# Pairing the half blocks of two tiles' mixer products, moving some evictions, and a new order, in a fused recurrence-and-mixer kernel

## The chip, the cores and the metric

The kernel runs on one core of one Trainium2 chip. The metric is the device time of one execution in microseconds (us); lower is better. Shown are the median and the spread of runs, and for one execution the hardware profile.

## The reference

Two stages follow each other. The first is a recurrence over 768 time steps for 4 batches and 8 heads of 40 values, with a 40 x 40 state per head. The second mixes over the tokens and over the 320 channels (8 x 40).

```python
for t in range(S):                                   # per batch and head
    y[t] = rt @ state
    Sa = state @ at
    state = state * wt[None, :] - outer(Sa, bt) + outer(vt, kt)
x = y as (batch, token, 320)
theta = x @ w_theta
zr, zi = x * cos(theta), x * sin(theta)
u = x + w_tok_r @ zr + w_tok_i @ zi                  # over the 768 tokens of a batch
out = u + max(u @ w_ch, 0)
```

All inputs and the output are float32.

## The kernel before

The 768 tokens of a batch are cut into 6 tiles of 128, so there are 24 tiles, numbered through the batches. Work on a tile has these stages; names in brackets are the tiles and the lines of the profile.

*Loads.* SP's queue issues six loads of 160 KB a tile (w, k, b, a, v at L358, r for two tiles at L367), into buffers for 2 to 6 tiles. GpSimd's queue loads the mixer's weights (L705, L708: w_theta and w_ch, in two pieces each, as three blocks of 128 rows of which the last is half empty) and the token weights (L717).

*Preparation, `prep`.* ScalarE takes log w (`lw`, L382). TensorE forms the running sums of the logs (L389) and sums of the heads (L395), ScalarE their exponential (`ex`, L399). VectorE adds `lw` once more (`sx`, L402) and ScalarE takes the exponential of that (`we`, L406): the decays before and after a step. GpSimd multiplies k, b and a by them (`kb` L413, `ah` L417) and casts v and r (L422, L442). For the first two tiles VectorE and ScalarE do that work. TensorE transposes the results (L339, L450), ScalarE copies them out of PSUM (`kbT`, `aT`, `vT`, `nuT` at L342, `rT` at L454).

*Scores.* Four times a tile, 8 products over 64 rows each (two heads lie in the two halves of the rows, `mode=64`) form a 128 x 1024 score block in two PSUM banks (L467), and VectorE multiplies it by a triangular mask on its way to SBUF (L472): `psi`, `phi`, `lamv`, `lamu`.

*Recurrence.* With `psi` and `phi`, TensorE solves for the tile (L500, L506, L518), ScalarE copies out (`nx` L512, `nu` L522), and the state `gt` goes on to the next tile (L539; VectorE L550 or L558, GpSimd L554). This is the chain from tile to tile within a batch.

*Readout.* TensorE forms the tile's outputs (L602 to L611), VectorE scales them into `x` (L618).

*Theta.* Three transposes of `x` (L582; 320 columns padded to 384), a copy by ScalarE (`xT`, L342), three products with w_theta (L627), a copy (`th`, L637). After a batch's tiles, ScalarE takes sines and cosines (`cs`, L651; a table load when the function set changes) and GpSimd multiplies by `x` (`zr`, `zi`, L663).

*Mixing.* A row block takes 12 products over the batch's tokens (L680), VectorE adds `x` (`u`, L687). Then, as for theta, three transposes (L582), a copy (`uT`), three products with w_ch (L627), and VectorE's last step (`oo`, L696) ahead of the store (L699).

Nothing is scheduled at run time. Each operation is entered with `add` in the order of the program, and is then emitted in the order of the list `ORDER`, which was made beforehand; each engine takes its own operations strictly in that order. `HOMES` gives each PSUM use its bank, and `WARM` places warm-up products (L774) of TensorE ahead of some operations. The engine of each operation is fixed where it is entered.

Of the kernel before, what the change touches and what calls it, by code (L numbers as in the profile page):

```python
# [19 lines left out]
FROM_POOL = 4  # L20
ORDER = [
    0, 5, 3, 6, 2, 1, 19, 20, 4, 21, 12, 22, 23, 34, 26, 25, 80, 35, 30, 10, 31, 24, 7, 28, 79,
    29, 8, 27, 38, 36, 40, 9, 39, 32, 33, 14, 105, 41, 81, 42, 82, 13, 43, 53, 83, 15, 84, 226,
    54, 89, 55, 106, 11, 56, 107, 58, 90, 227, 57, 16, 91, 59, 37, 85, 60, 229, 62, 108, 18,
    111, 86, 64, 63, 17, 92, 65, 110, 74, 228, 68, 109, 69, 44, 114, 112, 93, 115, 70, 76, 61,
    116, 71, 135, 117, 45, 124, 113, 136, 66, 125, 137, 67, 87, 46, 138, 120, 72, 88, 94, 121,
    47, 73, 211, 95, 139, 122, 75, 126, 96, 140, 159, 143, 118, 127, 144, 160, 130, 123, 145,
    187, 161, 146, 119, 77, 188, 164, 128, 212, 162, 189, 48, 147, 213, 165, 129, 190, 163, 195,
    180, 168, 166, 196, 214, 148, 197, 131, 198, 170, 216, 191, 171, 141, 169, 217, 132, 192,
    215, 176, 174, 265, 220, 142, 78, 175, 218, 149, 199, 221, 133, 150, 266, 167, 200, 222, 49,  # L30
    172, 177, 223, 193, 267, 50, 241, 318, 230, 242, 268, 232, 173, 270, 231, 243, 269, 201,
    236, 319, 194, 244, 271, 202, 245, 320, 181, 246, 274, 219, 233, 183, 293, 275, 249, 272,
    294, 178, 182, 321, 250, 224, 295, 179, 322, 276, 97, 296, 237, 225, 251, 277, 302, 252, 98,
    203, 134, 303, 151, 456, 204, 282, 280, 286, 152, 323, 283, 297, 253, 238, 325, 254, 304,
    281, 247, 368, 255, 184, 324, 248, 298, 256, 372, 239, 327, 369, 305, 257, 299, 329, 328,
    186, 234, 273, 330, 185, 235, 258, 373, 339, 240, 457, 278, 370, 348, 340, 288, 337, 371,
    306, 458, 279, 459, 462, 343, 349, 284, 307, 502, 300, 285, 460, 350, 461, 503, 287, 351,
    308, 301, 463, 352, 504, 338, 465, 309, 289, 353, 310, 326, 466, 333, 354, 505, 311, 344,
    467, 355, 484, 468, 334, 485, 346, 471, 336, 508, 331, 472, 356, 335, 464, 345, 486, 551,
    156, 473, 332, 357, 469, 487, 552, 474, 470, 507, 488, 506, 492, 553, 374, 511, 489, 493,  # L40
    292, 554, 341, 512, 509, 290, 532, 342, 555, 358, 153, 494, 533, 513, 359, 534, 556, 495,
    514, 360, 535, 521, 361, 99, 536, 522, 496, 558, 157, 541, 347, 557, 537, 475, 377, 523,
    497, 562, 538, 158, 291, 498, 476, 499, 560, 477, 563, 510, 542, 539, 379, 500, 561, 527,
    524, 154, 540, 375, 501, 543, 376, 579, 478, 381, 544, 490, 515, 491, 566, 580, 382, 479,
    100, 516, 155, 581, 545, 383, 101, 582, 480, 396, 567, 517, 583, 568, 380, 529, 397, 546,
    518, 598, 584, 378, 398, 519, 588, 528, 569, 599, 585, 589, 399, 600, 400, 647, 530, 547,
    559, 601, 401, 520, 102, 590, 402, 525, 548, 603, 591, 586, 628, 587, 648, 602, 604, 564,
    629, 549, 526, 572, 565, 630, 605, 649, 570, 631, 607, 482, 550, 650, 653, 609, 571, 608,
    637, 483, 592, 652, 638, 481, 610, 632, 651, 593, 639, 617, 633, 578, 654, 403, 594, 640,
    656, 404, 577, 595, 52, 103, 596, 531, 205, 104, 619, 597, 618, 51, 658, 694, 641, 659, 208,  # L50
    657, 384, 642, 385, 613, 386, 620, 695, 634, 387, 696, 643, 614, 606, 644, 697, 664, 615,
    662, 709, 665, 675, 616, 388, 623, 676, 635, 389, 636, 655, 677, 206, 390, 678, 573, 660,
    207, 611, 661, 710, 663, 612, 679, 575, 712, 645, 711, 209, 680, 574, 666, 646, 210, 621,
    681, 391, 622, 405, 392, 624, 259, 684, 698, 724, 685, 262, 682, 667, 725, 686, 826, 726,
    408, 727, 409, 406, 683, 410, 687, 728, 827, 729, 393, 828, 701, 411, 625, 412, 829, 413,
    394, 699, 830, 730, 414, 705, 576, 688, 731, 700, 706, 415, 260, 395, 831, 416, 703, 689,
    626, 263, 261, 732, 365, 264, 417, 739, 733, 362, 420, 421, 315, 422, 704, 423, 424, 738,
    832, 425, 734, 690, 426, 713, 312, 691, 418, 715, 735, 692, 702, 714, 427, 835, 428, 693,
    707, 716, 833, 736, 836, 429, 708, 627, 742, 366, 737, 430, 837, 363, 367, 741, 838, 668,
    717, 747, 364, 841, 745, 854, 718, 444, 855, 671, 316, 743, 746, 445, 856, 317, 446, 740,  # L60
    719, 313, 842, 857, 447, 862, 751, 858, 847, 863, 448, 314, 744, 843, 859, 864, 669, 449,
    844, 834, 432, 749, 433, 434, 670, 872, 435, 450, 750, 436, 865, 437, 902, 849, 748, 873,
    903, 766, 438, 874, 753, 767, 897, 904, 875, 768, 905, 752, 866, 921, 839, 673, 867, 769,
    876, 770, 968, 674, 771, 879, 840, 906, 772, 848, 754, 877, 969, 907, 755, 970, 922, 672,
    756, 878, 971, 923, 911, 757, 924, 972, 758, 850, 974, 759, 912, 868, 925, 439, 760, 860,
    908, 419, 1017, 845, 913, 869, 721, 846, 909, 861, 440, 881, 910, 887, 883, 720, 882, 870,
    914, 1018, 884, 973, 888, 871, 407, 1019, 451, 891, 890, 722, 1020, 893, 880, 889, 977, 892,
    915, 452, 852, 978, 975, 885, 894, 853, 453, 886, 979, 942, 949, 980, 927, 916, 895, 950,
    989, 898, 896, 778, 951, 926, 773, 779, 952, 723, 780, 454, 781, 990, 958, 782, 899, 959,
    930, 928, 774, 441, 931, 783, 900, 442, 983, 932, 953, 933, 784, 917, 960, 431, 954, 918,  # L70
    936, 1064, 961, 919, 851, 955, 761, 1065, 920, 1022, 984, 762, 443, 937, 1066, 956, 986,
    962, 993, 929, 985, 938, 963, 987, 1021, 943, 1067, 934, 1023, 957, 763, 939, 935, 998,
    1068, 945, 964, 1024, 1026, 999, 965, 764, 940, 1027, 944, 988, 1028, 1000, 775, 976, 1001,
    966, 1029, 901, 776, 981, 967, 802, 941, 814, 982, 1002, 995, 1196, 815, 991, 1003, 1034,
    1038, 992, 1069, 816, 817, 818, 1108, 1004, 819, 1044, 1035, 1007, 803, 947, 804, 1008,
    1045, 1070, 994, 820, 1009, 1046, 1032, 1109, 1010, 805, 948, 1025, 1073, 1071, 996, 1047,
    1074, 1030, 1033, 806, 1048, 807, 1115, 1043, 1075, 1031, 1011, 1076, 808, 946, 1049, 1012,
    1036, 1083, 1050, 997, 1197, 1084, 1051, 790, 1198, 1054, 1005, 1039, 1242, 791, 1201, 1055,
    1199, 792, 1006, 793, 1037, 1200, 1052, 1202, 1089, 1243, 1094, 1244, 1203, 1056, 1053,
    1040, 1085, 1245, 1095, 1205, 1086, 1079, 1207, 1041, 1206, 794, 1072, 1096, 1208, 795,  # L80
    1057, 1113, 1097, 1224, 1080, 1222, 1225, 1257, 785, 1081, 1223, 1211, 796, 1213, 786, 1212,
    1226, 1217, 1082, 1013, 1058, 1227, 455, 1098, 1014, 1059, 1247, 1232, 1291, 1228, 1219,
    1214, 1099, 1258, 1233, 1204, 1246, 1292, 1248, 1015, 1042, 1293, 1229, 1100, 1259, 1294,
    1234, 1111, 1272, 1016, 1091, 1101, 1260, 1077, 1249, 1251, 1273, 787, 1218, 1078, 1235,
    1354, 1274, 1252, 1087, 1275, 1110, 1253, 765, 1339, 809, 788, 1102, 1220, 810, 1088, 1114,
    1254, 1060, 1340, 1061, 1355, 1341, 1267, 1276, 1103, 1356, 1261, 1250, 1277, 1263, 1357,
    1092, 1230, 1342, 1281, 1231, 1262, 1062, 1297, 1282, 1236, 1090, 1063, 1104, 1278, 1255,
    1237, 1105, 797, 1256, 1283, 1269, 1264, 1344, 798, 1312, 1343, 1209, 1313, 1106, 1345, 777,
    1210, 1284, 799, 1107, 789, 1314, 1346, 1295, 821, 1279, 1221, 1315, 800, 1215, 1383, 1265,
    1216, 822, 1321, 1268, 1350, 1298, 1322, 1348, 1351, 811, 1280, 1266, 1349, 801, 1384, 1296,  # L90
    1316, 1093, 1385, 1285, 1112, 1317, 1360, 1386, 1323, 1271, 1389, 812, 823, 1286, 1136,
    1116, 1300, 1318, 1270, 824, 1238, 1324, 1137, 1347, 1239, 1302, 1301, 813, 1138, 1120,
    1240, 1303, 1361, 1325, 1388, 1241, 1117, 1352, 1287, 1122, 1326, 1306, 1308, 1288, 1307,
    1392, 1299, 1353, 1160, 1118, 1393, 1304, 1161, 1309, 1305, 1162, 1119, 1364, 1319, 1123,
# [96 lines left out]
def kernel(  # L191
# [91 lines left out]
    for i, t in sorted(to_zero, key=lambda e: e[0]):  # L283
        nc.vector.memset(t, 0.0)
# [526 lines left out]
```

## Time and profile before

| | before |
|---|---|
| median of 3 runs | 206.26 us (204.8 to 206.72) |
| profiled execution, span from first to last instruction | 204.3 us (the page gives no other time of it) |
| TensorE: matmuls / weight loads busy | 191.4 / 156.3 us |
| VectorE busy | 174.4 us |
| ScalarE busy | 151.6 us |
| GpSimd busy | 127.0 us |
| granted TensorE clock, mean | 1.000 |
| DMA, moved | 30.82 MB, mean 151 GB/s |

A busy time is the union of an engine's instructions; matmuls overlap each other, and their ends are modelled, so TensorE's busy share says less than the distance from one start to the next. An engine that is idle and isn't waited for costs nothing. The chain that ended last follows the execution back from its end, at each step to what released it.

### The profile page before, as it was taken

How to read it: one execution, taken by the hardware profiler on the slowest of the kernel's cores; microseconds unless marked ns; L12 is line 12 of the kernel's file. 1: busy time of each engine (PE TensorE's matmuls, PEld its weight loads, DVE VectorE, ACT ScalarE, POOL GpSimd, SP SyncE). 2: the span in 40 equal slices, each digit the busy share in tenths (PEclk: the TensorE clock that was granted, in tenths of full speed). 3: DMA queues.
4: the chain of work that ended last, by engine and by line, in shares of the span. 5: the costliest groups of instructions: out<-in, count | busy, mean ns of one | idle time of the engine just before them, and what ended most of it. 6: DMA issues, size and time to landing. Idle time of an engine off the chain costs nothing.

```text
span 204.3 us, 8134 instructions
## 1 busy us (share of the span) xinstructions
PE 191.4 (94%) x3372; PEld 156.3 (77%) x3372; DVE 174.4 (85%) x277; ACT 151.6 (74%) x364; POOL 127.0 (62%) x186
## 2 busy tenths in 40 slices
PE   7878789888999999999899999999999999999993
PEld 6756668667878888887678888788888878777771
DVE  7499899799999998996886989999999987956543
ACT  3577668799999977868667859898999967756021
POOL 3015178559999996659959918548987953635000
PEclk9999999999999999999999999999999999999999
DMA  6989899999899999979999889797999400012223
GB/s 135 198 158 197 155 172 167 182 159 195 139 186 204 155 256 191 147 141 178 170 191 207 169 176 186 169 181 131 220 199 192 96 3 5 0 67 78 87 77 116
DMA packets 134181, 30.82 MB, mean 151 GB/s; under 512 B 125824, under 2 KB 134144, under 8 KB 134144
## 3 DMA queue, kind: packets, MB, share of 16 engines
q1 hardware_dynamic: 131712, 27.54, 68.8%
q0 software_dynamic: 2432, 2.77, 8.6%
q8 instruction: 26, 0.43, 0.9%
q14 instruction: 11, 0.09, 0.1%
HBM read 29.13 MB, written 3.93 MB: 162 GB/s over the span
## 4 chain that ended last, share of the span: by engine, by line
PE 71%; DVE 8%; DMA 8%; SPq 5%; ACT 2%; issue 2%; POOL 1%; DVEq 0%; ACTq 0%; POOLq 0%
PE ps_s L680 19%; PE ps_s L339 12%; PE ps_d L467 10%; PE ps_s L627 9%; SPq L358 4%; DMA wrow_i<-in_moe_w_tok_i_dram 4%; PE ps_s L582 4%; DMA raw_v<-in_v_dram 3%; PE ps_s L450 2%; PE ps_s L539 2%; DMA raw_r<-in_r_dram 2%; PE ps_s L518 2%; PE ps_s L611 2%; PE ps_s L725 2%; PE ps_s L506 2%
## 5 line engine op out<-in xcount | busy, mean ns | idle before, releaser
L413 POOL TENSOR_TENSOR kb<-raw_kb,ex 128x320 bf16<-128x320 f32 x44 | 37.6, 868 | 10.0 <-ACT ex L399 4.3
L680 PE MATMUL ps_s<-zr,wtok_r 128*128 128x320 bf16 x144 | 41.1, 299 | 0.0
L680 PE MATMUL ps_s<-zi,wtok_i 128*128 128x320 bf16 x144 | 41.0, 299 | 0.0
L472 DVE TENSOR_TENSOR psi<-ps_d,mask_p 128x1024 bf16<-128x1024 f32 x24 | 29.2, 1216 | 4.3 <-PE ps_d L467 4.1
L472 DVE TENSOR_TENSOR lamu<-ps_d,mask_p 128x1024 bf16<-128x1024 f32 x24 | 29.1, 1215 | 3.0 <-PE ps_d L467 2.9
L472 DVE TENSOR_TENSOR phi<-ps_d,mask_n 128x1024 bf16<-128x1024 f32 x24 | 29.2, 1215 | 0.8 <-PE ps_d L467 0.8
L472 DVE TENSOR_TENSOR lamv<-ps_d,mask_p 128x1024 bf16<-128x1024 f32 x24 | 29.0, 1215 | 0.5 <-PE ps_d L467 0.4
L417 POOL TENSOR_TENSOR ah<-raw_a,we 128x320 bf16<-128x320 f32 x22 | 19.1, 868 | 8.0 <-issue 5.0
L663 POOL TENSOR_TENSOR zr<-cs,x 128x320 bf16<-128x320 f32 x23 | 18.0, 791 | 6.7 <-DVE oo L696 4.2
L663 POOL TENSOR_TENSOR zi<-cs,x 128x320 bf16<-128x320 f32 x23 | 17.9, 790 | 6.2 <-ACT cs L651 6.2
L467 PE MATMUL ps_d<-aT,kbT 64*128 64x128 bf16 x384 | 17.3, 217 | 1.8 <-ACT aT L342 1.1
L342 ACT COPY uT<-ps_s 128x192 f32<-128x192 f32 x24 | 7.6, 324 | 14.6 <-PE ps_s L582 14.6
L554 POOL TENSOR_TENSOR gt<-sum,ex 128x320 bf16<-128x320 f32 x13 | 9.4, 725 | 13.3 <-DVE sum L550 13.3
L680 PEld LDWEIGHTS <-wtok_r 128*128 128x128 bf16 x144 | 14.0, 97 | 4.1
L687 DVE TENSOR_TENSOR u<-ps_s,x 128x320 bf16<-128x320 f32 x24 | 11.6, 486 | 5.9 <-PE ps_s L680 5.7
L342 ACT COPY kbT<-ps_s 128x512 f32<-128x512 f32 x24 | 14.3, 594 | 3.1 <-PE ps_s L339 2.9
L680 PEld LDWEIGHTS <-wtok_i 128*128 128x128 bf16 x144 | 14.1, 98 | 3.3
L442 POOL CAST r<-raw_r 128x640 bf16<-128x640 f32 x11 | 8.0, 725 | 11.7 <-ACT lw L382 9.7
L696 DVE SCALAR_TENSOR_TENSOR oo<-ps_s,u 128x320 f32<-128x320 f32 x24 | 11.6, 484 | 4.2 <-PE ps_s L627 3.5
L467 PEld LDWEIGHTS <-kbT 64*128 64x128 bf16 x384 | 11.5, 94 | 4.8 <-ACT kbT L342 1.9
L339 PE MATMUL ps_s<-ident,kb 128*128 128x128 bf16 x192 | 14.7, 219 | 0.4 <-POOL kb L413 0.2
L609 PE MATMUL ps_s<-kb,lamv 128*128 128x40 bf16 x192 | 15.1, 180 | 0.0
(119 smaller groups left out, 590.8 us busy)
## 6 DMA issues: line engine op xcount, KB each, us to landing
raw_w<-in_w_dram SPq DMA_DIRECT2D x24, 160.0 KB, 4.2
raw_r<-in_r_dram SPq DMA_DIRECT2D x24, 160.0 KB, 3.6
raw_a<-in_a_dram SPq DMA_DIRECT2D x24, 160.0 KB, 3.5
raw_kb<-in_b_dram SPq DMA_DIRECT2D x24, 160.0 KB, 3.8
raw_kb<-in_k_dram SPq DMA_DIRECT2D x24, 160.0 KB, 3.9
raw_v<-in_v_dram SPq DMA_DIRECT2D x24, 160.0 KB, 4.2
out_dram<-oo SPq DMA_DIRECT2D x24, 160.0 KB, 2.4
wrow_i<-in_moe_w_tok_i_dram POOLq DMA_DIRECT2D x6, 192.0 KB, 5.3
```

The lines of the kernel that those rows point to most:

```text
L339: nc.tensor.transpose(out=dst[:, c:c + 128], in_=pair(src, g), identity=ident)
L342: nc.scalar.copy(out=out.bitcast(FP32), in_=in_)
L413: lambda j=j: (nc.vector if fast else nc.gpsimd).tensor_tensor(out=paired(kb[:, j])[:, :, :, 0:D], in0=natural(raw_kb[s4][:, j]), in1=invW ...
L417: lambda: (nc.vector if fast else nc.gpsimd).tensor_tensor(out=paired(ah)[:, :, :, 0:D], in0=natural(raw_a[i % 6]), in1=Wi, op=ALU.mult),
L467: nc.tensor.matmul(t[:, q, g, :], lhsT=lhs[rows(q), g * 128:(g + 1) * 128], rhs=rhs[rows(q), g * 128:(g + 1) * 128], start=True, stop=True)
L472: add("DVE", kindm, i, lambda: nc.vector.tensor_tensor(out=dst.rearrange("p a b c -> p (a b) c"), in0=ps(p).rearrange("p a (g c) -> p (a g ...
L609: nc.tensor.matmul(o, lhsT=lamv[:, p, g, :], rhs=kb[:, 0, h, 0:D], start=first, stop=False, skip_group_check=True)
L627: nc.tensor.matmul(dst, lhsT=lhs[:, kt, :], rhs=rhs[:, kt, :], start=kt == 0, stop=kt == 2)
L663: nc.vector if fast else nc.gpsimd).tensor_tensor(
L680: nc.tensor.matmul(ps(pk)[:, 0:DM], lhsT=wtok[nm][:, s, j * 128:(j + 1) * 128], rhs=zs[c][:, s], start=n == 0 and c == 0, stop=n == NT - 1 ...
L687: add("DVE", "uadd", q, lambda: nc.vector.tensor_tensor(out=u[:, 0:DM], in0=ps(pk)[:, 0:DM], in1=x[:, 0:DM], op=ALU.add), 488, [pk, ("x", ...
L696: add("DVE", "oo", q, lambda: nc.vector.scalar_tensor_tensor(out=oo, in0=ps(ck)[:, 0:DM], scalar=0.0, in1=u[:, 0:DM], op0=ALU.max, op1=ALU ...
```

## The change

Pairs: the outputs `x` of two tiles in turn lie side by side in one tile `xp` of 640 columns, and so do `u` (`up`). 640 columns are five transposes of 128: two blocks of the first tile, two of the second, and one that holds the last 64 columns of the first tile in its upper half of rows and the first 64 of the second in its lower half. One copy takes all five out of PSUM. Each tile then has two full products, and the shared block gives each of the two a product over 64 rows, from its half of the rows into its own PSUM bank. The mixer weights are held in five blocks to match: the first three as before, with the lower half of the third now filled with rows 0 to 63, and rows 64 to 319 as two more. They take four loads each instead of two. Tiles 22 and 23 go alone, as before, from `xs` and `us`.

Decay sums: for tiles 0 to 6 (`EXCLUSIVE = 7`) a TensorE product of `lw` with the strict triangle `mask_p` gives the earlier sums themselves, and ScalarE takes their exponential from PSUM; VectorE's `sx` falls away for them.

Alternatives: an operation can carry a second way of doing it on another engine (`alts`), and a list `PICK` says which take it. A masked eviction's second way is a plain copy with sign on ScalarE followed by a triangular select on GpSimd, in place. In the built kernel 21 of 96 go that way (9 `phi`, 8 `lamv`, 3 `psi`, 1 `lamu`). 33 copies out of PSUM go to VectorE (13 `nuT`, 8 `vT`, 5 `kbT`, 4 `aT`, 3 `uT`) and 5 of `xT`; 7 of 12 token-weight copies go to ScalarE; 14 z products are on VectorE (2 before); 3 more casts of v are on ScalarE.

The lists `ORDER`, `HOMES` and `WARM` are new (63 warm-up products, 65 before). Sines are taken for tiles 0 to 3, then 4, then 5 of the last batch (0 to 2, 3 and 4, then 5 before). Part of the memsets move from VectorE to GpSimd.

The core of the diff:

```diff
+        for n in PICK:
+            self.ops[n].eng, self.ops[n].fn = self.ops[n].alts[0]
...
+        if i < EXCLUSIVE:
+            xk = ("ps", "cx", i)
+            add("PE", "cx", i, lambda: nc.tensor.matmul(
+                ps(xk)[:, 0:DM], lhsT=mask_p[:, 0, :], rhs=lw[:, :, 0:D], start=True, stop=True),
+                mm(320), [("lw", s2)], [xk], new=(xk, 1), tail=tail(320))
+            add("ACT", "ew", i, lambda: nc.scalar.activation(
+                out=we, in_=ps(xk)[:, 0:DM], func=AF.Exp), 455, [xk], [kw], table="lnexp")
...
         add("DVE", kindm, i, lambda: nc.vector.tensor_tensor(
-            out=dst.rearrange("p a b c -> p (a b) c"),
-            in0=ps(p).rearrange("p a (g c) -> p (a g) c", c=128),
-            in1=mask.to_broadcast([128, 2 * G, 128]), op=ALU.mult), 1217, [p], [dkey])
+            out=flat, in0=whole(), in1=mask.to_broadcast([128, 2 * G, 128]), op=ALU.mult),
+            1217, [p], [dkey], alts=(("ACT", lambda: nc.scalar.mul(
+                out=flat, in_=whole(), mul=sign)),))
+        add(None, "sel", i, None, 0, [dkey], [dkey], alts=(("POOL", lambda: nc.gpsimd.affine_select(
+            out=flat, in_=flat, pattern=[[0, 2 * G], [1, 128]], compare_op=ALU.is_gt,
+            fill=0.0, base=0, channel_multiplier=-1)),))
...
+    def blocks_of(t):
+        if t.shape[-1] == 3 * 128:
+            return [t[:, m:m + 128] for m in (0, 128, 256)]
+        return [t[:, m:m + 128] for m in (0, 128, DM + 64, DM + 192, 256)]
...
+    def mixed(kind, q, lhs, wt, wkeys, lkey, at="tile"):
+        for c in range(1 if alone(q) else 2):
+            pk = ("ps", kind, q + c)
+            def go(c=c, pk=pk):
+                n = 3 if alone(q) else 2
+                for kt in range(n):
+                    nc.tensor.matmul(ps(pk)[:, 0:DM], lhsT=lhs[:, c * n + kt, :],
+                                     rhs=wt[:, 3 * c + kt, :], start=kt == 0,
+                                     stop=kt == 2, skip_group_check=n == 2)
...
+        def both():
+            for c in range(2):
+                nc.tensor.matmul(ps(("ps", kind, q + c))[:, 0:DM], lhsT=lhs[rows(c), 4, :],
+                                 rhs=wt[rows(c), 2, :], start=False, stop=True,
+                                 skip_group_check=True)
...
-    def mix3(dst, lhs, rhs):
-        for kt in range(3):
-            nc.tensor.matmul(dst, lhsT=lhs[:, kt, :], rhs=rhs[:, kt, :],
-                             start=kt == 0, stop=kt == 2)
```

## The prediction

> **What bounds the kernel now.** I read the page first, then the table by ten-microsecond stretches, the chain that ended last, the timeline where TensorE changes between forms of product, the groups by line, and the order in which each engine and queue gets its instructions.
>
> Two lines of the page's slices, TensorE and VectorE (each digit is the busy share of 5.1 us):
>
> ```profile
> PE   7878789888999999999899999999999999999993
> DVE  7499899799999998996886989999999987956543
> ```
>
> The stretches (busy us of PE, PEld, DVE, ACT, POOL, then granted clock, DMA share, GB/s):
>
> ```profile
> 10.00:20.00 10.00, 7.67 (x152) 6.00 (x144) 9.24 (x12) 7.71 (x19) 3.59 (x5) 1.00 0.91 174
> 40.00:50.00 10.00, 8.77 (x181) 7.00 (x179) 9.47 (x11) 9.65 (x21) 7.58 (x11) 1.00 0.98 181
> 60.00:70.00 10.00, 9.88 (x190) 8.01 (x188) 10.00 (x16) 9.25 (x21) 9.46 (x15) 1.00 1.05 185
> 150.00:160.00 10.00, 10.00 (x204) 8.61 (x202) 9.79 (x16) 9.46 (x23) 8.00 (x11) 1.00 1.01 200
> 160.00:170.00 10.00, 10.00 (x157) 7.98 (x156) 8.76 (x11) 7.24 (x18) 7.55 (x12) 1.00 0.05 15
> ```
>
> There are three regimes. Until about 50 us the DMA engines are full and TensorE has holes: it waits for tiles to arrive. From 50 us on TensorE has none to speak of, while VectorE, ScalarE and GpSimd are nearly full too until 80 us. After 160 us the loads are over and TensorE works off a backlog. The clock is 1.00 throughout.
>
> A busy TensorE is not proof, so I price its steps from two lines of the chain (start, length, work) and three of the timeline (start, length, operation):
>
> ```profile
> 90.16 0.45 PE ps_s L339 x8
> 165.92 1.91 PE ps_s L680 x14
> ```
>
> ```profile
> 161.75 0.33 PE L582 MATMUL ps_s<-ident,x 128*128 128x128 bf16 x3
> 162.01 0.62 PE L467 MATMUL ps_d<-aT,kbT 64*128 64x128 bf16 x16
> 162.56 0.62 PE L339 MATMUL ps_s<-ident,kb 128*128 128x128 bf16 x8
> ```
>
> A transpose of 128 columns takes 0.056 us (0.45/8), a product of 320 columns 0.136 (1.91/14). The score products use 64 rows each and run two at a time. Three transposes from 161.75 should make room at 161.92; the scores start at 162.01, and their 16 (8 pairs of 0.053, 0.43) hold the next work until 162.56. So one stretch of 64-row work costs about 0.09 on entry and 0.12 at the end, together 0.2 us more than its products. Steps of 80 columns take 0.035, shorter ones 0.025.
>
> Adding TensorE's order at these steps gives 181.9 us for the kernel before. Set against the last L518 product of a tile, whose tile-0 time is 12.7 us with 6.6 us of work ahead of it, the lag (time less work) is 6.1 us at tile 0, 14.9 at tile 5 (49.4 us), 16.0 at tile 8 (65.0) and 18.4 at tile 23 (178.9). After that product 21.4 us of work are left and the span is 204.3, so 4.0 us are lost at the end. The lag arises almost wholly before 50 us; afterwards TensorE's own work is the time. That is the sum I use: 181.9 + 18.4 + 4.0 = 204.3. The page gives no other time of this execution; the three runs shown lie 0.5 to 2.4 us above the span, their median 206.26 about 2.0 above, and I add 2.0 at the end.
>
> **The change on TensorE.** Eleven pairs of tiles, in theta and channel mixer each, make 22 pair operations; tiles 22 and 23 keep the old way. (1) Five transposes replace six: 22 x 0.056 = -1.2 us. (2) A pair had six full products; it now has four, and two half blocks of 64 rows side by side. 44 full products go (-6.0), 22 side-by-side pairs come (+3.0): -3.0. That two 320-column halves overlap is not in this trace; the bounds are 0.136 a pair (as the score pairs overlap) and 0.272 (not at all, total 0.0). I take the first, since the score products use the same row halves and separate PSUM banks, and so do these. (3) Each pair would open a 64-row stretch, but in the built order 18 of the 22 stand beside score products; stretches go from 64 to 58: 6 x 0.2 = -1.2. (4) Seven early decay sums become a product (L389 form): +7 x 0.136 = +1.0. (5) Two fewer warm-up products: -0.1. Sum -4.5; added up in the built order TensorE has 177.4 us instead of 181.9.
>
> The Trainium skill (TensorEngine Tiling, Key Properties) says that changing the tiling mode drains TensorE, which speaks against a change that adds 22 mode changes of its own. The rows agree, with 0.2 us a stretch. By that rule with each pair alone the term would be +4.4 instead of -1.2, and the whole TensorE sum +1.1; the built order, with 18 joined, is why I don't take it.
>
> **The other engines.** *VectorE*: 21 of 96 masked evictions (L472, 1.215 us) leave, -25.5; 7 decay sums (L402, 0.482), -3.4; 7 of 12 token-weight copies (L729, 0.551), -3.9; about -3 of memsets, most of them in the first 5.4 us. It gains 13 nuT, 8 vT, 5 kbT, 4 aT and 8 xT/uT evictions, priced by L729 (768 words of 16 bits in 0.551; 512 then between 0.37 in proportion and 0.55; I take 0.42, with a fixed part), +17.6; 12 of the z products (0.485), +5.8; one ah, +0.5. Sum -11.9. *ScalarE*: 21 evictions of 1024 columns; copies of 256 and 512 words take 0.378 and 0.594, so 0.16 + 0.85 a thousand gives 1.03 each, +21.6; 48 xT/uT copies become 18 (-8.1); the copies that VectorE took -12.5; seven token copies +3.4; two table loads fewer -2.6; small ones +1.9: +3.7. *GpSimd*: 21 masks by select, in no row at this size. Bounds: the rate of the cast (320 in 0.451, 640 in 0.725), 1.05 us, and that of the two-input product L413 (320 in 0.868), up to 2.6; the 128-column select that builds masks takes 0.29, and scaled up from there it is 1.1 to 1.7. I take 1.35: +28; four more weight loads and the memsets +5, twelve z products fewer -9.5, the rest -2.5: about +21, to 148 of some 200 us. By the Trainium skill (GPSIMD Engine Reference, Performance versus the Vector engine: 1.03 to 1.8 cycles an element for one input at 1.2 GHz) a select would be an estimated 0.9 to 1.5 us; the sum would stay as it is.
>
> None of these is counted as time: GpSimd's 21 us fall in a queue that was idle for 77, ScalarE's 3.7 in 53 idle. That cover fails where selects queue ahead of kb and ah products in 50 to 80 us, where GpSimd was 96% busy; but in its built queue the first five selects stand ahead of that stretch, where it was idle for 22 of 50 us, and the first batch's z products come before the sixth, with four of twelve given to VectorE.
>
> What a moved mask does add is latency. A mask was one operation of 1.215 us; now it is 1.03 on ScalarE, then a select of 1.05 to 2.6: +0.9 to +2.4 on the way to x0 (psi) or nu (phi), 12 such in all, with every later eviction on ScalarE and kb product on GpSimd queued behind. VectorE's shorter queue gives some of it back. I put the part that TensorE feels at +1.0 (bounds: -2, the shorter queue wins; +10.4, all twelve show at the low price).
>
> **The load-paced start.** There a saved product is only a longer hole, so what counts is when a tile's data are there. Of 144 loads of 160 KB on SP's queue, in the old order the last that batch 0 (tiles 0 to 5) needs for its recurrence is the 42nd, issued at 39.0 us; in the new one the 39th. At 0.93 us a load that is -2.8. Past that the places match within two (tile 7: 49th in both; tile 9: 59th and 61st). Against it, theta's weights are loaded twice (200 KB more early, at 170 GB/s +1.2). The new first tile also doesn't wait behind memsets for its decay:
>
> ```profile
> 4.70 0.45 DVE L284 MEMSET x<- 128x32 uint32 x10
> 5.41 0.43 DVE L402 TENSOR_TENSOR sx<-ps_s,lw 128x320 f32<-128x320 f32 x1
> ```
>
> but that second is swallowed by the loads behind it. Net -1.6 at tile 5 (bounds 0 and -4): its L518 at 47.8 instead of 49.4.
>
> **Sum.** From tile 5 on: 177.4 - 34.3 = 143.1 us of TensorE work (147.4 before), 3.5 of later lag (18.4 - 14.9), 4.0 at the end, +1.0 for the masks. 47.8 + 143.1 + 3.5 + 4.0 + 1.0 = 199.4 of span, 4.9 less; with 2.0 around it **201.4 us**.
>
> **Rivals.** *A, more gain*: VectorE, full from 10 to 80 us, is what holds the early tiles, not the loads; then its 4.2 us less work up to tile 6's x (58.0 to 53.8 by the rows) come through in place of the 1.6, and the shorter queue pays for the masks: 201.4 - 2.6 - 1.0 = 197.8. For it: 9.2 to 10 us busy in each of those stretches. Against: DMA share 0.91 to 1.05 in the same ones. *B, slower*: the moved psi and phi masks are on the recurrence, and TensorE, which takes its work in order, stands at L506 and L518 for each. At the low price 12 x 0.87 = 10.4 instead of 1.0: 210.8. At 0.08 a mask it is the forecast's 1.0; past 0.67 us a mask (1.0 + 4.9 of gain + 2.1 over 12) the kernel is slower than before by over 1%. For it: twelve waits in a strict order with only a few us of slack on three full engines. Against: in the old trace DVE is as full there, so a mask waited in its queue anyway. *C, no change by the loads*: DMA share averages 0.96 up to 160 us; if the loads set tile 23's time, TensorE's saving becomes idle time: 204.3 + 2.0 = 206.3, and the 0.4 MB more of weights would take another 2.4 at 170 GB/s only if no buffer wait of the loads absorbed them. Against: tile 23's last load is issued at 156.9 us and its L518 comes 22 us later, where tile 7 needed 11 (46.2 to 57.7), so there are some 10 us of slack. *D, the change doesn't do what it says*: half blocks don't overlap, +3.0: 204.4.
>
> **Chances.** Forecast 0.48 (own range 199 to 204), A 0.18, B 0.15, C 0.12, D 0.07. A measurement of this kernel can tell about 1%, 2.1 us. Faster by over 1% (under 204.2): forecast and A, 0.66. Within 1%: C and D, 0.19. Slower: B, 0.15. The range reaches into A below and halfway to B above: 195.5 to 208.
>
> **What would show it.** Right: two L627-like half products starting within 10 ns of each other and taking 0.136 a pair; VectorE near 163 us busy; selects of 1.1 to 1.7; TensorE's work near 177 with tile 5's nu product near 48 us, lag under 19 at the last. Wrong: waits of L506 or L518's weight loads on the selects of over 5 us in total (B); the last nu tracking the last load's landing (C); selects over 2 us with kb products behind them.

## The result and the profile after

The changed kernel takes 211.99 us (median, 210.14 to 213.62), the old one 206.24 beside it: a ratio of 1.028 (95% interval 1.021 to 1.036). It is slower, where 201.4 was forecast. The profiled execution took 211.76 us, 210.1 of them span.

TensorE and VectorE in the slices of the changed kernel's page (each digit the busy share of 5.25 us):

```profile
PE   6997897998879898899999999999999899997993
DVE  4279897999978997789899879799989997468353
```

```profile
40.00:50.00 10.00, 8.74 (x173) 6.72 (x170) 9.02 (x12) 9.04 (x20) 7.60 (x11) 1.00 0.98 180
50.00:60.00 10.00, 8.78 (x180) 6.99 (x177) 9.29 (x12) 8.14 (x21) 7.65 (x11) 1.00 0.98 165
60.00:70.00 10.00, 8.29 (x167) 7.21 (x167) 8.73 (x13) 9.42 (x21) 8.77 (x13) 1.00 1.04 202
80.00:90.00 10.00, 8.77 (x185) 7.45 (x182) 7.35 (x11) 7.70 (x20) 8.58 (x14) 1.00 1.18 204
150.00:160.00 10.00, 9.51 (x216) 8.31 (x212) 9.12 (x14) 9.51 (x22) 9.74 (x14) 1.00 0.54 135
160.00:170.00 10.00, 9.38 (x169) 7.22 (x166) 9.69 (x14) 9.27 (x18) 8.14 (x11) 1.00 0.41 91
```

These are six of the stretches, with columns as in the prediction. The old kernel's TensorE had next to no holes from 50 us on (9.88 busy at 60 to 70 us); the changed one has them until 90 us (8.29 busy at 60 to 70 us) and again from 150 us. Until 90 us no other engine is full in the stretches shown (at most 9.42 of 10); from 150 to 170 us GpSimd and VectorE nearly are (9.74, 9.69). So TensorE waits, for several things in turn. Its waits, over the whole span (us in total, times, longest):

```profile
PE ps_s L357 <- POOL kb L394: 1.8, 4, 0.7
PE ps_d L496 <- ACT aT L360: 1.7, 2, 1.1
PE ps_s L765 <- DVE oo L788: 1.2, 1, 1.2
...
PE ps_d L496 <- ACT phi L508: 1.0, 1, 1.0
```

The chain that ended last, between 50 and 92 us (start, length, work), shows what stands behind GpSimd's ah and kb: loads.

```profile
57.99 3.99 DMA raw_a<-in_a_dram
62.05 0.10 issue
62.15 0.86 POOL ah L394
...
77.14 3.49 DMA raw_kb<-in_b_dram
80.67 0.08 issue
80.77 0.87 POOL kb L394
```

The halves do overlap. A pair of half products is a line with x2 in TensorE's timeline; the next product starts 0.25 us after it, one step of 0.136 and the changes of form:

```profile
189.62 0.31 PE L662 MATMUL ps_s<-wch,uT 64*128 64x320 bf16 x2
189.87 0.31 PE L765 MATMUL ps_s<-zr,wtok_r 128*128 128x320 bf16 x1
```

Among the groups (busy us, mean ns) there is one surprise, VectorE's mixer products at L751. The moved masks (L508, L510) are shown beside them:

```profile
L751 DVE TENSOR_TENSOR zr<-cs,xp 128x320 bf16<-128x320 f32 x8 | 6.8, 869 | 0.0
L751 DVE TENSOR_TENSOR zi<-cs,xp 128x320 bf16<-128x320 f32 x4 | 2.6, 657 | 0.0
L751 DVE TENSOR_TENSOR zi<-cs,xs 128x320 bf16<-128x320 f32 x2 | 2.0, 1016 | 0.0
L510 POOL TENSOR_SCALAR_AFFINE_SELECT phi<-phi 128x1024 bf16<-128x1024 bf16 x9 | 10.4, 1150 | 0.9 <-ACT phi L508 0.9
L508 ACT ACTIVATE phi<-ps_d 128x1024 bf16<-128x1024 f32 x9 | 9.3, 1037 | 0.3 <-PE ps_d L496 0.3
```

The same instruction took 0.48 to 0.49 us in the old trace, where VectorE did two of them:

```profile
L663 DVE TENSOR_TENSOR zi<-cs,x 128x320 bf16<-128x320 f32 x1 | 0.5, 491 | 0.8 <-ACT cs L647 0.8
L663 DVE TENSOR_TENSOR zr<-cs,x 128x320 bf16<-128x320 f32 x1 | 0.5, 479 | 0.0
```

**The prediction's sum, refilled.** I add up TensorE's order at the prediction's steps, with 0.1 us for each change between full and 64-row products, in both traces: 182.6 us before, 178.0 after, so 4.6 less (forecast 4.5; the prediction's own count was 181.9 and 177.4). The rest is the lag.

| part of the span, us | forecast | after | before, same count |
|---|---|---|---|
| tile 5's last nu product | 47.8 | 49.9 | 49.4 |
| TensorE's work behind it | 143.1 | 143.6 | 147.9 |
| lag gained from there to tile 23's (masks with it) | 4.5 | 10.8 | 3.1 |
| lost at the end | 4.0 | 5.8 | 3.9 |
| span | 199.4 | 210.1 | 204.3 |

Of the 10.8, 6.7 arise between tiles 5 and 11 (49.9 to 90.9 us), 2.5 between tiles 19 and 23 (150.0 to 181.3 us).

### The profile page after: what moved, and what is told of

It reads as the page before. It is cut to its first block, busy times and chain, and to the rows that moved or that the text cites. A ratio compares the mean times of both kernels' runs of the same rounds, so it can differ in the third digit from the quotient of the medians.

```text
span 210.1 us, 8112 instructions
## 1 busy us (share of the span) xinstructions
PE 192.0 (91%) x3355; PEld 153.9 (73%) x3355; DVE 170.3 (81%) x268; ACT 155.5 (74%) x335; POOL 144.8 (69%) x204
## 4 chain that ended last, share of the span: by engine, by line
PE 51%; ACT 13%; DMA 11%; DVE 10%; issue 5%; POOL 5%; SPq 4%; POOLq 0%; DVEq 0%; ACTq 0%
PE ps_s L765 15%; PE ps_s L357 8%; PE ps_d L496 6%; PE ps_s L652 4%; DMA raw_kb<-in_b_dram 3%; DMA raw_kb<-in_k_dram 3%; SPq L374 2%; DMA wth<-in_moe_w_theta_dram 2%; PE ps_s L620 2%; DMA raw_a<-in_a_dram 2%; PE ps_s L662 2%; DVE zr L751 2%; DVE oo L788 2%; POOL kb L394 1%; PE ps_s L555 1%
## 5 line engine op out<-in xcount | busy, mean ns | idle before, releaser
L506 DVE TENSOR_TENSOR psi<-ps_d,mask_p 128x1024 bf16<-128x1024 f32 x21 | 25.6, 1217 | 4.4 <-PE ps_d L496 4.3
L394 POOL TENSOR_TENSOR ah<-raw_a,we 128x320 bf16<-128x320 f32 x21 | 18.5, 880 | 6.4 <-DMA raw_a<-in_a_dram 1.7
L506 DVE TENSOR_TENSOR lamv<-ps_d,mask_p 128x1024 bf16<-128x1024 f32 x16 | 19.5, 1216 | 0.3 <-PE ps_d L496 0.2
L496 PE MATMUL ps_d<-aT,kbT 64*128 64x128 bf16 x384 | 16.9, 221 | 2.2 <-ACT aT L360 1.7
L506 DVE TENSOR_TENSOR phi<-ps_d,mask_n 128x1024 bf16<-128x1024 f32 x15 | 18.2, 1214 | 0.5 <-PE ps_d L496 0.5
L752 POOL TENSOR_TENSOR zi<-cs,xp 128x320 bf16<-128x320 f32 x18 | 14.3, 809 | 4.3 <-ACT cs L737 4.3
L689 PE MATMUL ps_s<-kb,lamv 128*128 128x40 bf16 x192 | 15.1, 180 | 0.0
L772 DVE TENSOR_TENSOR up<-ps_s,xp 128x320 bf16<-128x320 f32 x22 | 10.7, 488 | 5.4 <-PE ps_s L765 5.3
L691 PE MATMUL ps_s<-kb,lamu 128*128 128x40 bf16 x192 | 14.8, 179 | 0.1
L427 ACT ACTIVATE ex<-ps_s 128x328 f32<-128x328 f32 x24 | 10.5, 450 | 5.5 <-PE ps_s L423 3.8
L549 ACT CAST nx<-ps_s 128x320 bf16<-128x320 f32 x24 | 10.3, 431 | 5.5 <-PE ps_s L543 5.3
L357 PEld LDWEIGHTS <-kb 128*128 128x128 bf16 x192 | 12.2, 100 | 2.9 <-POOL kb L394 2.4
L483 ACT COPY rT<-ps_s 128x512 bf16<-128x512 bf16 x24 | 13.3, 598 | 1.3 <-PE ps_s L479 1.3
```

The lines of the kernel that those rows point to most:

```text
L357: nc.tensor.transpose(out=dst[:, c:c + 128], in_=pair(src, g), identity=ident)
L394: pool = ("POOL", lambda: nc.gpsimd.tensor_tensor(out=dst, in0=in0, in1=in1, op=ALU.mult))
L427: got = add("ACT", "exp", i, lambda: nc.scalar.activation(out=ex, in_=ps(pk)[:, 0:DM + 8], func=AF.Exp), 440, [pk], [kex], table="lnexp")
L483: add("ACT", "er", i + x, lambda x=x: nc.scalar.copy(out=rT[:, x].rearrange("p (g t q) -> p g t q", g=G, q=8), in_=ps(pr).bitcast(BF16).re ...
L496: nc.tensor.matmul(t[:, q, g, :], lhsT=lhs[rows(q), g * 128:(g + 1) * 128], rhs=rhs[rows(q), g * 128:(g + 1) * 128], start=True, stop=True)
L506: add("DVE", kindm, i, lambda: nc.vector.tensor_tensor(out=flat, in0=whole(), in1=mask.to_broadcast([128, 2 * G, 128]), op=ALU.mult), 1217 ...
```

## The experiments

The kernels e1 to f4 ran on one chip, g1 and g2 on a second, g5 to h2 on a third, k1 to k4 on a fourth, each set with the old kernel timed beside it. "Lag" is TensorE's time less its work, as in the prediction, read from one profiled execution at the last nu product of tiles 5, 11 and 23 and at TensorE's last product ("end"). For e2 none is given.

The expectations name their theories by letters: M, the moved masks are late; S, supply, the data come late from the DMA engines; O, the new order makes TensorE wait for other engines; Z and P, VectorE's z products are stretched beside GpSimd and hold up what is queued behind them.

| kernel | us | ratio to the old one, interval | lag 5 / 11 / 23 / end |
|---|---|---|---|
| old (first trace) | 206.24 | 1 | 14.7 / 15.9 / 17.8 / 18.3 |
| changed (first trace) | 211.99 | 1.028 [1.021, 1.036] | 15.5 / 22.2 / 26.3 / 28.6 |
| e1 masks back | 224.72 | 1.086 [1.079, 1.093] | 18.8 / 27.3 / 39.5 / 43.5 |
| e2 weights once | 215.49 | 1.038 [1.031, 1.045] | |
| e3 no alternatives | 244.55 | 1.183 [1.174, 1.191] | 25.0 / 36.1 / 53.5 / 58.5 |
| e4 pairs in old order | 253.03 | 1.222 [1.215, 1.230] | 20.1 / 26.6 / 56.7 / 66.0 |
| f1 changed | 213.21 | 1.039 [1.030, 1.047] | 13.8 / 22.1 / 27.7 / 30.1 |
| f2 changed, r left out | 207.54 | 1.010 [1.003, 1.017] | 13.5 / 18.3 / 21.6 / 24.0 |
| f3 old, r left out | 204.36 | 0.996 [0.993, 0.998] | 14.2 / 15.4 / 17.0 / 17.4 |
| f4 changed, z on GpSimd | 219.40 | 1.068 [1.060, 1.076] | 15.1 / 24.8 / 32.6 / 34.7 |
| g1 changed, r, a, v left out | 207.51 | 1.002 [0.999, 1.005] | 14.3 / 19.1 / 21.9 / 24.2 |
| g2 old, r, a, v left out | 204.92 | 0.990 [0.986, 0.994] | 13.5 / 14.7 / 16.5 / 16.9 |
| g5 changed, no selects | 211.52 | 1.031 [1.024, 1.037] | 17.3 / 22.2 / 25.9 / 28.3 |
| g6 as g1, no selects | 206.28 | 1.003 [1.000, 1.006] | 13.7 / 18.5 / 20.8 / 23.1 |
| h1 as g1, half masks | 205.98 | 1.003 [1.000, 1.006] | 13.2 / 17.1 / 19.3 / 21.7 |
| h2 as g2, half masks | 203.78 | 0.994 [0.991, 0.997] | 13.3 / 14.2 / 16.5 / 16.9 |
| k1 changed | 215.93 | 1.047 [1.042, 1.051] | 14.6 / 22.8 / 28.8 / 31.2 |
| k2 changed, z of one input | 212.86 | 1.031 [1.024, 1.037] | 17.4 / 23.7 / 28.4 / 29.4 |
| k3 as g1 | 208.64 | 1.009 [1.006, 1.013] | 15.7 / 20.5 / 23.3 / 25.7 |
| k4 as g1, z of one input | 203.38 | 0.985 [0.981, 0.990] | 14.6 / 17.5 / 19.5 / 20.4 |

TensorE's work by the same count is 178.0 us in every one with the new order; only the lag moves. The three runs of the unchanged new kernel spread from 1.028 to 1.047, so a verdict below is read within one chip where there is a partner on it. For g5 and g6 there is none.

**Undoing moves: e1, e3, e4, f4.** The first idea was that the moved masks' longer way (theory M) is what costs.

```diff
e1  PICK without the 21 masks and their selects (VectorE does all 96)
e3  PICK = []          (no operation takes its second way)
e4  EXCLUSIVE = 0; PICK = []; ORDER near the old one, pairs at their second tile's place
f4  PICK without the mixer products z (GpSimd does all but the last tile's)
```

> The changed kernel with its 21 moved masks back on VectorE (same order, same places, everything else as changed). TensorE's own work is the changed kernel's (178.0 us at the steps of the prediction, against 182.6 before); its lag is 27.8 against 17.9. Theory M (the two-engine masks are late and TensorE stands for them): the lag falls by more than 4 us, time 204 to 208. Theory S (tiles' data come late, DMA-bound until about 100 us) and theory O (the new order and the moved copies and z products): no gain; VectorE gets 25.5 us more on top of 170, so 212 to 218.

> The changed kernel with none of the operations moved to another engine (masks, copies out of PSUM, z products, casts all on their first engine), in the new order. Theory M: 204 to 209, the masks' waits go. Theory O in its form that the moved copies and z products cost time: faster than with the masks alone back. Theory O in its form that the order itself is at fault, or that it needs the moves: slower than the changed kernel, 213 to 220, VectorE and ScalarE standing in each other's way. Theory S: 211 to 214.

> The old order with only the pairs taken over: paired x and u, five transposes, four full and two half products, four weight loads; decay sums, engines and the order of everything else as before, each paired operation standing where its second tile's stood, halves beside score products where they are near (77 stretches of 64-row work, 64 before and 58 in the changed kernel). TensorE's work: -4.2 for the pairs, +2.6 for 13 more stretches, so -1.6. Theory S: +1 to +3 for the weights' loads less the 1.6, 206 to 208. Theory O (the new order is at fault, pairs are not): 204 to 206. A theory that the pairs themselves are at fault (theta late by a tile, PSUM banks held longer): 209 or more.

> The changed kernel with the z products back on their first engine (13 from VectorE to GpSimd, one the other way), the rest as changed. In the changed kernel z products on VectorE took 0.66 to 1.02 us where the last tile's took 0.48 to 0.49 before. Theory Z (two-input products on VectorE are slowed by GpSimd and hold up the rows, 1.4 us of it at the last row block): 209.5 to 211. Theory O in the form that the order needs every move: 213 to 217, GpSimd 10 us busier.

All four are slower than the changed kernel (213.21 on the same chip, f1), by 6 to 40 us, and e1, e3 and f4 are slower than any theory allowed. With the masks back TensorE waits for VectorE's masks and sums instead (e1, whole span):

```profile
PE ps_d L494 <- DVE phi L504: 2.9, 4, 1.1
PE ps_s L355 <- POOL ah L392: 1.9, 2, 1.7
PE ps_s L689 <- DVE lamu L504: 1.8, 1, 1.8
```

So theory M falls: in the new order the moved masks save time. But these runs say little more, since an order and its choices are made for each other. In e4 TensorE's work came to 181.0 as expected, but by the two lists at least 31 operations outside the pairs stand at other places too, and its longest waits are for ScalarE (4.2 us for one `gd`, 3.0 for one `th`). Whether the pairs themselves cost time there is not shown. In e3 and e4 the granted clock was also 0.50 for 24 and 31 us of the span (last section).

**Second weight loads: e2.** Paired tiles need part of each mixer weight again on other rows.

```diff
-    nc.gpsimd.dma_start(out=to, in_=part)
+    nc.gpsimd.dma_start(out=to, in_=part) if c < 2 else nc.gpsimd.memset(to, 0.0)
```

> The changed kernel without the second copy of the mixer weights: the four extra pieces are filled by memsets on GpSimd in place of loads (0.4 MB less to move; the paired tiles' outputs are then not the reference's). Theory S, with the extra loads as its main part: 2.4 us of DMA time at 170 GB/s less, all of it ahead of 90 us, and TensorE's holes there close by as much: 209 to 210. Theories M and O: within 0.7 us of the changed kernel, 211.5 to 212.5.

1.038 [1.031, 1.045] against f1's 1.039 [1.030, 1.047] on the same chip: no gain is seen, though one below some 2 us would not show. The 2.4 us that theory S put on these loads lie at the edge of what the two intervals leave room for, so they are at most a small part of the loss.

**Supply: f1 to f3, g1 and g2.** Fewer loads, the same instructions on the five engines, on both kernels.

```diff
f2, f3  loads of r                  only for i < 4
g1, g2  loads of r only for i < 4, of a and v only for i < 6
```

> The changed kernel itself, as the measure for the others of this set on the same chip. Every theory: 211 to 213, 5 to 6 us over the kernel before.

> The changed kernel with r loaded for tiles 0 to 3 alone; later tiles use what the buffers hold (outputs of those tiles are not the reference's). A sixth of the loads is gone, so the DMA engines, full until 140 us, have 3.2 MB less to move (18 us at 175 GB/s). Theory S (TensorE waits for tiles that come late): the lag gained between 55 and 90 us (5.5 us over the kernel before) goes, and the kernel comes to 202 to 207, at or below the kernel before with the same loads taken away. Theory O (the new order makes TensorE wait for other engines, whatever the loads): 210 to 212, and 4 us or more over the kernel before without these loads.

> The kernel before with the same loads of r taken away. Theory S says that loads set its first 50 us too: 200 to 203. Theory O, and the reading of its trace that TensorE has no holes after 60 us: 203 to 206.

> The changed kernel, with r loaded for its first four tiles only and a and v for their first six: the later tiles' products read what the buffers hold, so the outputs of those tiles are other ones; every instruction of the five engines stays. Loads per tile fall from 6 (r as two halves for two tiles, one a tile) to 3. Theory S (what is left of the difference, about 3 us once r was not loaded, is still the supply of data): another 3 us fall away, 204 to 205 us, level with the old kernel under the same treatment or up to 4 us below it, since TensorE has 4.6 us less to do. Theory O (the new order makes TensorE wait for products, copies and masks of the other engines, whatever the loads do): the time stays near 206 to 207 us, about 3 us above the old kernel under the same treatment, and the lag still jumps by over 1.5 us at tile 8 on a product of GpSimd.

> The old kernel with the same loads left out (r beyond four tiles, a and v beyond six; outputs of the later tiles are other ones). Leaving out r alone took 1.3 us off it. Both theories: another 0 to 1.5 us off, 203 to 204.5 us; it is the partner of the run before it. Under theory S the two are level or the changed one is shorter, under theory O the changed one is 3 us longer.

Without r the changed kernel gets 5.7 us shorter, the old one 1.3: of the 7.6 us between them on that chip 4.4 go. Without a and v too, 2.6 us are left on another chip (207.51 less 204.92), about as many as without r alone (3.2). So supply is 4 to 5 us, shown, and the rest is not supply. (k1 and k3 below give 7.3 on a further chip, 5.2 after taking off the 2.1 by which the old kernel got shorter beside g2. In f1's profile some 1.5 us of it are a lower clock behind a late load; see the last section.) In f1 the chain names one place, tile 9's a (my expectations say tile 8; counted in the trace it is the tenth ah product):

```profile
56.93 4.87 DMA raw_a<-in_a_dram
...
61.97 0.86 POOL ah L394
62.83 0.05 issue
62.87 0.47 PE ps_s L357 x4
```

It is the 58th load on SP's queue (the 55th in the old order), issued at 56.9 us and landing at 61.8 (52.4 and 55.7 in the old one; why it is issued so much later was not tried), and TensorE stands 1.9 us for the product made of it. With little supply (g1) TensorE stands 0.4 us at this place. Both kernels draw at about the same rate there (165 to 202 GB/s at a DMA share near 1, 50 to 70 us), and in the old one TensorE doesn't wait for a product of GpSimd there at all.

Which load bites changes from execution to execution. The wait for tile 9's ah was 0.4 us in the first trace and 0.5 in k1, where a kb product cost 3.0 instead. And f1 has a second place, late in the span, which k1 shares (1.7 us) and the first trace hardly (0.5): GpSimd stands for a load of r, and the `gt` queued behind the cast comes late. These are TensorE's two longest waits in f1, and GpSimd's timeline:

```profile
PE ps_s L357 <- POOL ah L394: 1.9, 1, 1.9
PE ps_s L357 <- POOL gt L591: 1.9, 1, 1.9
```

```profile
151.88 0.72 POOL L400 CAST r<-raw_r 128x640 bf16<-128x640 f32 x1 [4.05 <-DMA raw_r<-in_r_dram]
```

**Selects and masks: g5, g6, h1, h2.** In g5 and g6 the 21 blocks are written as zeros, since unmasked ones would drive theta far out of the sine's range.

```diff
g5, g6  in_=whole(), mul=0.0 * sign   and no affine_select
h1, h2  masked evictions on VectorE from tile 2 on: 4 of 8 heads
```

> The changed kernel with all its loads and without the 21 selects of GpSimd; the 21 score blocks that ScalarE copies are written as zeros, so that nothing needs masking (outputs are other ones). This takes 21 x 1.10 to 1.15 us = 24 us off GpSimd. Theory S: tiles 8 to 11 wait for loads anyway and the time falls by 0 to 2 us, ratio to the old kernel 1.02 to 1.035. Theory O in its GpSimd form: 4 us or more fall away, ratio 1.015 or less, and the wait for GpSimd's ah of tile 8 goes.

> As the run before it, and besides with the loads of r beyond four tiles and of a and v beyond six left out, as in the run that came to a ratio of 1.002. If GpSimd's selects are what is left of the difference, the ratio falls to 0.985 to 0.99 (the old kernel under the same treatment came to 0.990); if it is VectorE's or ScalarE's work or the fixed order itself, it stays at 0.997 to 1.003.

> The changed kernel with the same loads left out, and with VectorE's masked evictions from the third tile on done for one half of the eight heads only (the other half keeps an older tile's values; outputs are other ones). About 67 of them shrink from 1.2 to some 0.65 us: VectorE loses about 37 us of its 170. If VectorE's late results are what keeps TensorE's saving from showing (theory O in its VectorE form), TensorE's lag ends near 18 instead of 24 us and the ratio comes to 0.975 or less, below the old kernel under the same treatment; if it is ScalarE's copies or GpSimd's products, the lag ends over 22 us and the ratio stays above 0.99.

> The old kernel with both of these treatments, the partner of the run before it: 88 masked evictions shrink by about 0.55 us each, VectorE loses some 48 us of its 182. The old kernel's TensorE waits little after tile 8, so its time falls by 0 to 1.5 us, ratio 0.982 to 0.99. Theory O in its VectorE form: the changed kernel, with 4.6 us less TensorE work, is then the shorter one of the two; otherwise the old one stays shorter by 2 us.

Taking 22 us off GpSimd (144.8 to 122.6 busy in g5) moves the ratio by nothing that can be told: 1.031 lies within the 1.028 to 1.047 of the unchanged kernel, and 1.003 (g6) within the 1.002 to 1.009 of g1 and k3. Those ran on other chips, so a gain of some 2 us would not show. Taking a fifth off VectorE (170.2 to 137.5 in h1) leaves the two kernels 2.2 us apart (h1 less h2), against 2.6 with it (g1 less g2, another chip). The lag falls more (h1 21.7 at the end, g1 24.2, the old kernel 16.9 in both), but h1's profiled execution was its shortest. So the amount of work on VectorE or GpSimd is not the main answer either, and my expectation for h1 under a VectorE cause (0.975, lag near 18) failed.

**One input instead of two: k1 to k4.** g1's trace had the hint: one z product of 1.92 us, and one of TensorE's two longest waits behind it. k3, the same kernel on another chip, has it again. VectorE's and GpSimd's timelines there:

```profile
62.03 1.93 DVE L752 TENSOR_TENSOR zi<-cs,xp 128x320 bf16<-128x320 f32 x1
63.88 0.48 DVE L699 TENSOR_TENSOR xp<-ps_s,we 128x320 bf16<-128x320 f32 x1
```

```profile
61.48 0.79 POOL L753 TENSOR_TENSOR zr<-cs,xp 128x320 bf16<-128x320 f32 x1
62.23 0.71 POOL L592 TENSOR_TENSOR gt<-sum,ex 128x320 bf16<-128x320 f32 x1
62.90 0.71 POOL L401 CAST r<-raw_r 128x640 bf16<-128x640 f32 x1
```

The product starts while GpSimd works, and ends 0.35 us after the third GpSimd instruction in a row (63.96 against 63.61). The xp behind it is read from PSUM, is not slowed (0.48), but ends at 64.37, and TensorE, which needs its bank, starts 40 ns later. So the experiment takes the second SBUF input away and leaves the engine, the order and the length:

```diff
-  nc.vector.tensor_tensor(out=dst, in0=in0, in1=in1, op=ALU.mult)
+  nc.vector.tensor_reduce(out=dst, in_=in0.rearrange("p (m o) -> p m o", o=1),
+                          op=ALU.max, axis=mybir.AxisListType.X)
```

> The changed kernel again, as the partner on this chip for the run after it: ratio 1.028 to 1.039 as before.

> The changed kernel, with the 14 mixer products that it computes on VectorE (line 751) done as a copy-like reduction that reads cs alone, with the second input left out (outputs are other ones). GpSimd's products and selects stay. Theory P: what is left beside the loads is that VectorE's products of two SBUF inputs stand still while a GpSimd instruction runs (0.48 to 1.6 us each in the traces, mean 0.87) and push what is queued behind them on VectorE. Then these 14 fall to 0.4 to 0.5 us and the time by 1 to 3 us against the run before it. If the products' delay is hidden, the time stays within 0.8 us.

> The changed kernel with r loaded for four tiles and a and v for six, again, as the partner on this chip for the run after it: ratio 1.002.

> The same with little supply, where one of these products took 1.92 us at 60.6 us of the span and TensorE then stood 1.36 us for the xp that was queued behind it. Theory P: that wait goes, TensorE's lag at tile 8 falls from 17.4 to 16 us and at the end from 24.2 to 21 to 22.5, the ratio from 1.002 to 0.985 to 0.995 (the old kernel under the same treatment: 0.990). If another engine's result comes last in the same places, the ratio stays over 0.998.

With all loads 3.1 us fall away (215.93 to 212.86), with few loads 5.3 (208.64 to 203.38). The first figure is the less sure one, because loads land differently each time: in k1's trace TensorE stood 3.0 us for one kb product behind a load of 7.1 us, in k2's 1.0 at most for a kb product. The groups of k4:

```profile
L752 DVE TENSOR_REDUCE zr<-cs 128x320 bf16<-128x320 f32 x8 | 3.7, 479 | 0.0
L752 DVE TENSOR_REDUCE zi<-cs 128x320 bf16<-128x320 f32 x6 | 2.8, 479 | 0.0
```

TensorE's waits after 50 us, k3 first, then k4:

```profile
PE ps_s L357 <- DVE xp L699: 1.4, 2, 1.2
PE ps_s L766 <- DVE oo L789: 1.2, 1, 1.2
PE ps_s L766 <- DVE zr L752: 0.7, 2, 0.5
PE ps_s L766 <- ACT wtok_r L825: 0.6, 1, 0.6
```

```profile
PE ps_s L768 <- ACT wtok_r L827: 0.6, 1, 0.6
PE ps_s L357 <- ACT kbT L360: 0.4, 1, 0.4
```

The 14 products take VectorE 6.5 us instead of 11.8, and the first three waits of k3 are gone or down to 0.2. The wait for oo went with them: in k3 three z products of about 1 us (187.9 to 190.9) stood ahead of the oo that frees a bank for the last rows. The granted clock is 1.00 in both traces until 201 us, so it has no part in this. That is theory P, shown by its removal. It doesn't follow that the products belong back on GpSimd: there they cost 6 us more (f4, GpSimd 152.5 us busy), and the waits of that run were not taken apart.

The Trainium skill (SBUF — State Buffer, Who interferes with whom) has this as a rule: a VectorE instruction with two SBUF inputs shares a read port with GpSimd, and one blocks the other for a whole instruction, while a `tensor_reduce` never does. The rows agree: 0.479 for each reduction, 0.48 to 1.93 for the products. The 1.93 is more than one instruction's block; it spans three of GpSimd's.

With both causes out, the changed kernel (k4, 0.985 [0.981, 0.990]) is level with the old one with the same loads left out (g2, 0.990 [0.986, 0.994], another chip), or shorter by some 1 us; TensorE has 4.6 us less to do. Its lag at the end is still 3.5 us longer (20.4 against 16.9). The waits that stand in its trace (0.6 us for wtok_r at 82.7, 0.4 at 60.1, and smaller ones) were not tried apart, and neither was a version that computes the whole output with the z products' second input in another place than SBUF.

## Why the prediction was wrong

*TensorE's work: right.* 4.6 us less where 4.5 was forecast; in 21 of the 22 pairs the halves start 3 to 4 ns apart and cost one step; the change of form costs 0.1 on entry and 0.1 after, also for a pair alone.

*Prices on the other engines: mostly right, one badly wrong.* Selects took 1.09 to 1.12 us and two of them 1.35 (1.35 taken), mask copies on ScalarE 1.03 in the mean (1.03), nuT copies on VectorE 0.414 (0.42), GpSimd 144.8 us busy (148). (The 38 copies that VectorE gains come to 16 to 17 us at the prediction's own prices, not 17.6; nothing hangs on it.) VectorE has 170.3 against some 163. The step that failed is "12 of the z products (0.485), +5.8": that row came from two products at the very end of the old kernel, where GpSimd was idle. In the new place 14 of them take 11.4 us instead of 6.8, and the seven kb and ah products 5.1 instead of 3.4. Those two make 6.3 of the 7.3 us.

*"None of these is counted as time": wrong, and this is the larger error.* The cover was idle time summed over 50 us and more; but each engine takes its instructions in order, so one stretched product delays the xp or oo behind it and TensorE with it. The runs put 3.1 us on it with all loads, 5.3 with few, where the sum had nothing.

*The later lag, 3.5 us: wrong.* I carried it over from the old order as if it belonged to the kernel. It belongs to an order and the times at which its data come; the new order's was 10.8 with the masks, and 4.9 in k4.

*The load-paced start, -1.6: not borne out.* The last load that batch 0 needs was issued three places earlier and landed 2.2 us earlier (41.5 us against 43.7), but tile 5's last nu product came at 49.9 us, and at 48.2 and 49.1 in f1 and k1, against 49.4 before: from 0.5 later to 1.2 earlier. So the earlier load alone didn't bring tile 5 forward by as much, and what paces it stays open. The costlier step is what came after it: I had compared the places of tiles 7 and 9 in the queue with the old order's and found them within two, but not set them against the time at which the new order uses them. Tile 9's a landed at 62.0 us, and TensorE was there first. Here the supply of 4 to 5 us begins, for which the sum had no term behind tile 5.

*The masks, +1.0:* not told apart in size. TensorE waits 1.0 us for one phi copy of ScalarE (the last of the waits shown), no weight load waits over 0.3 us for a select, and without any select the ratio is the same as far as chips can be compared (g5, g6).

*Rivals.* B named a number close to the result (210.8), but not its cause: its sign, 5 us of waits for the selects ahead of x0 and nu, is missing. That its total came near is luck. A falls with the result, and halving VectorE's masks brought little. C named the loads, but as what paces the last tile: tile 23's last nu product comes nearly 21 us after the last load is issued (160.6 to 181.3), and the loads bite earlier, between tiles 5 and 11 and, in f1 and k1, near 157 us. D falls with the halves' 3 to 4 ns. That a product changes its price with the engine it runs on beside GpSimd was in none of them.

## What to carry to other kernels

When work is moved between engines, price it where it will run: a VectorE product of two SBUF inputs took 0.83 us in the mean of 14 beside a busy GpSimd, not its 0.485 alone, and what counts is who is queued behind it. A lag measured in one order isn't a constant that a new order inherits, so set each load's landing and each evicted tile's end against the place where TensorE will ask for it. And when engines are 70 to 90% busy, take away one suspect at a time, on both kernels and on one chip: here the busy time that looked like the cause (masks, selects) was not the main part of it, and late loads and products of two SBUF inputs were.

## What the runs showed that I had not expected

- VectorE's product can wait for several GpSimd instructions in turn (1.93 us for one of 0.48), and GpSimd's own products stretch too beside VectorE's (1.03 to 1.04 for two of the last zr at 188 to 190 us of k3, 0.80 to 0.81 in k4).
- The granted clock can fall where TensorE has waited. In e4 it is 0.66 at 50 to 60 us (first line; columns as above), in f1, the unchanged new kernel, 0.83 at 60 to 70 us (second line). In the traces it is 1.00 or 0.50: in f1 it is 0.50 from 63.1 to 66.5 us, right behind the wait for tile 9's ah, and TensorE does 1.95 us of work (by the prediction's steps) in those 3.41. By this estimate some 1.5 us go there on top of the wait; that the wait set it off is not shown. In the changed kernel's first profile the clock is 1.00 in all stretches but the last (0.94 from 200 us on), so there it is no part of the loss. What sets it off stays open: in k1 TensorE stood 3.0 us for a kb product at 56 to 58.9 us, and the clock stayed at 1.00 there.

```profile
50.00:60.00 10.00, 7.61 (x132) 6.46 (x133) 6.00 (x7) 8.26 (x19) 9.88 (x14) 0.66 1.04 182
60.00:70.00 10.00, 8.06 (x147) 7.13 (x145) 7.86 (x12) 7.44 (x14) 7.00 (x11) 0.83 1.01 201
```
